# Two interleaved recurrent-memory transformer layers: full V passes for blocks 0, 1 and 14, spread weights copied from partition 64, and a new order of tasks

## The chip, the cores and the metric

The kernel runs on one NeuronCore of a Trainium2 chip. The metric is the device time of one execution in microseconds. The kernel before took 1785.24 us as the median of three runs (1784.02 to 1785.46). Engines are named as in the profile: PE is TensorE (PEld its weight loads), DVE VectorE, ACT ScalarE, POOL GpSimd, SP SyncE. SP and POOL mostly issue DMAs here.

## The reference

The input is one sequence of 2048 tokens of width 512, and the same layer is applied twice, with the same weights. A layer adds a recurrent-memory attention to its input, and then a gated feed-forward network (FFN). In the attention the sequence is cut into 64 segments of 32 tokens; 8 memory rows go ahead of each segment, and the attention's output for these rows is the memory of the next segment, so segments must follow one another.

```python
mem = mem0                                        # 8 x 512
for s in range(64):
    h = concat([mem, x[:, 32*s:32*s+32]], axis=1) # 40 rows, x after layernorm
    q, k, v = h @ Wq, h @ Wk, h @ Wv              # 32 heads of 128
    p = softmax(where(mask, q @ k.T * scale, -1e9))
    o = (p @ v) @ Wo
    mem = o[:, :8]; outs.append(o[:, 8:])
# one layer, applied twice:
x = x + attention(layernorm(x))
h = layernorm(x)
x = x + (sigmoid(h @ w_gate) * (h @ w_up)) @ w_down   # 512 -> 1792 -> 512
```

All inputs are bfloat16.

## The kernel before

**Steps.** Both layers run at once, the second six segments behind the first (`LAG` = 6), so that 70 steps do the whole work. In 58 of them both layers are present and every matmul of the step has 80 columns (40 rows of each layer); the 6 first and 6 last steps have one layer and 40 columns. A step (`emit_step`) goes through 32 heads in groups of six: Q and K (L890), their copy out of PSUM to `qku` (ACT), scores (L904), the mask added (DVE, L918), maximum, subtraction, exponential (ACT, L928), sum, reciprocal and product to `pb` (DVE, L923 to L935), a transpose on PE (L947), a spread of the transposed probabilities into `ptsb`, probabilities times V (PV, L973), a copy to `otsb` (ACT), and Wo (L991). At the end of the step DVE writes the new memory rows into the next step's `hT`, and ACT writes the segment's output to `oxT`.

**The spread.** A transposed pair of heads (u, 16 + u) lies in PSUM with the one head's keys at partitions 0 to 39 and the other's at 64 to 103. `ptsb` has for each pair two stretches of columns: stretch 0 is used with partitions 0 to 39, stretch 1 with partitions 64 to 103, and the rest of each is zero, so that one matmul takes both heads' keys at once. Stretch 0 is a plain copy of partitions 0 to 39. Stretch 1 is written on partitions 0 to 103, each multiplied by a scalar of its partition, `lower`, that is 0 below partition 64 and 1 from there on: on ACT an activation with a scale (L1222), on DVE a product (L1224). In a plain copy the lines are L1230 (ACT) and L1232 (DVE).

**V.** V of the memory rows and of the 8 last or first rows of a segment is computed inside the steps, as strips: 32 columns of `hT`, four matmuls side by side on PE (`strips`, L815). V of the other 24 rows of a segment doesn't depend on the memory and is computed ahead, for a block of 4 segments, written to DRAM (`scr`) and read back by the steps into `vsb`. A `v_pass` (L693) multiplies a tile of 128 columns by all of Wv in 32 matmuls of 512 columns; a block has only 96 such columns, so columns of other blocks fill up the rest. `v_half` (L730) does the same with 64 columns, two matmuls side by side; `v_strip` does it with 32 columns. Before the first steps `v_group` makes V of blocks 2, 14, 3, 4, 5, 7 and then 8, 10, 11, 13 of layer 0; what blocks 0 and 1 still need is made in between by one strip and one half (`trace`, L1150). In layer 1, a block's V is made when its FFN of layer 0 is done: `v_pass` with fillings from layer 0, but a half for block 14 and a strip for block 15. In the start the results are staged in nine buffers of the FFN's weight rings (`wd`, `wg`, `wu`: `bootp`), from which SP and POOL write them to DRAM (L1226).

**FFN.** When a block's four segments are done, `ffn` transposes `oxT` (L1061), adds the input, normalizes (`layernorm_T`, L642: statistics L649, transposes L662), and does gate and up (L1093), tanh (L1098), product (L1100) and down (L1117). Its weights are streamed from DRAM for each block by POOL (L1085, L1086, L1111).

**What sets the order.** `Kern` doesn't issue instructions but tasks, with an engine or a choice of ACT or DVE, a duration, and what they read and write. `Planner` plays them through with fixed costs and gives each engine the ready task of highest rank. The ranks are written out: a compressed list, `SEQUENCE` (L53 to L152), holds the rank of every task, and the lines that read it are

```python
for k, (q,) in enumerate(struct.iter_unpack("<H", code)):
    T[left.pop(q)].tail = -float(k)
```

So which of ACT and DVE does a copy, and in what order all engines work, comes from `SEQUENCE` and the planner's costs. PE tasks that the planner sees starting late get filler matmuls on the tile `hot` in front of them (`warm`, L416; issued at L1216); the first ones are at the start of the kernel. A semaphore wait stands only where data or a buffer demands it.

Of the kernel before, what the change touches and what calls it, by code (L numbers as in the profile page):

```python
# [53 lines left out]
;Aht@pIrb8fB#p5?Q#$k*OKvZZTq^c3OM%bV44b=*R*ZTyW=(F)eXpo=!dnjd%&eFWe?4v9B9J-6{(d-LCut;#!E)o@XKL;|1Yh}DX~>av(XnTcNY5yDmuUNDYpk)1hbP~Icf*@B%SY3<$N!PMdC+w  # L54
TzC*H?wh$B-*Ih~y~Z^1eU45ybkQ1*)!rl+2M7#!1kA=M>_00gM+A4yerPR?|M?Mj6^>>JOVW=CEf+cd3@>&Nfi0vId6NWR);FU?#N7i-E<e}?kQ5;smk7+$yR>6M$&vA+ka>GT!8=_b4-#fP#)eF7
^yFAVNqaBx;!Z*DxPH}w4u4hwLD|Xk-(55Lk^B_BDfkRj%d!v=C<*w7SG;+fg+&T)>)vE^_U=fY&kC>YwKQIya^N!=lH>FlpJ`Jr&lF|=A)fY+g;i{E@r#X;(VDk3V2MMXacuh+Y1k_asM6Wlyelal
#hat)UmCRL92k7baU(yGZ`~C!81W~7P5Erk>AYc<Vay?}YFcMj2ofpnp$(sP&YA3~nf~n+b1fFy?|Zym`QSa144a*IfxPvGj&Q1ek!IqLN$jiF41N6_7PG1D?N__fhI#wYegIrLSdO>RI&L#ADzYcB
9Qqa8r^xHgLyr2s6(Q^~qr%E_$NJ+TpJ_bc{R>AcDm>XZ4K<5#ddGdVwMU;&cRuZ|Sp~k`OZ$e|X_~sQ@384vzE1LEOy7FI`;?xf^#@MMQ)L6bC_!Zn4S4CHx9Vjn^H}pFj3R+|IJ2mzre;noNVd$S
`{%;vED%u54cw3M^F8VWNicF9{B~XUq?7A1595()pJ)9U7U(TRXvIYfie-lrSI2C)aZ1BBh3$_bQ;!I-B=8ScYh1ck&O!bB=K^(6{|r6Qx~A%7Guq$r@Iax)(DGfYMGmfWTtN`TiNx0^a_h-)zaQ;Y
Bg~_fxFI1YgW5VrkU}+v(OG0q+i!<|tAlPcRfvDusTf+wG<zAh-6L;+Y1?sI#2|g1{X&hwViH*}otG=?Uzck!7(XzcfK!b2s0y$`SNOr$pn;5(vR*N@6t6GIu9c&BiE<wNN?P(QqaXRd3M2ScK!LD`  # L60
7NE8fpYJ@UG|VxPeYSAG0la_&djDUlCG|bBoZOzAT#$(zHi(qOLpXAuXb5%<ke>jX1k1`o2(mU?ngq;3!G;hMQLm2&9MTEUYd^USvXFM#vQ$cKmjg>LrQvGCuN0;hmD;jcN{gk}oA#{rr~t7er6x;>
4TAPsm6b5FLH-g|Nf9h4giYb{D&c`|4)4`L+JTg9TM;~}=IotkUY(*Y!dPX~EqzNqLnvA&8*(y?XY|Ec+`KUE@_SSE)gkFi<&UF6JtvvpbP{*<I0G^z6$#&pA}^v95^Q4FK#<`jp&L`QSey9`{hytp
ep4|DPRnnzJfR5<$bbinu=f`jwczBNxe3uhZ<*z*5#J~4a?5s>6axJof)V}FxLuSWLQ`X$p%|GAo3ni>PtV+JzEAC$o%TiCe#d7B$K5bY%WL%|Y?`a4x@DA(YsP8dw{qC8hys!6@G=TJ3;?U)VFlx0
p<M<>KJllT(z)CRu8?`e3^R_R7%q?S32qi7rh98c7=(LFh!0=aD^hH1fNfXqg+Sja7$z4P_WGLKlHYlxk!E{x!eD5T8C@MZ?8P+s8nOs}&1S4ol`b-NnC>Xi=go6~%Yjg-4mHO!zq-ODIoX(~$HahI
@>xN0b)~I`DIDj5VKMa;CZ!v*mkbmOJ)#~W9x(W_v;<nswK`+PTq}ipg*!qKSltnE+$xw7Xt>R@wAQgZ(cg;enc1@7fR_`9(15bKuOa8wjwP|W7E?oWno808^?XT*fvZ96JauH_vO6Tmg0YAX{%<GP
x&vaN_I%f%_>nw(eGPl2kX+vA>jgyX^`O19337j8ctxfD{|+Geiw9%@3fRrZv?20mB-ZcAf?E$T01iSEPFlGkD*OepKVV{in{2e29t=mMTqiEZTBE&ID`7X6Mk+WhT~yUj_1`*B0!BsL3UYqo?S%Vq
U~wE&tp6ZiVbg<Vu#-btWwj?J)D@CYb1QP&m*#PL94pnFvBWYRVkl3T5;SG{PpgL>Y&7Ql1a;Xg%4O>TI04XhhFijc@Xaj9&%wm+O^!e2Is7ho@U?|Mv)s#Z>S-JQQ#^hP6vJ~o=FQdi%0==QiO4>}
e22-8{8_Hk?+)?_0!^US$Hin*eL}LmU1~LxfMwEBA4T-2y4BQI`Q`64rb)aYczym_%e@Wk1AuUFK%C=ysBJZCRbO!Y(YYGT<zd6Mwt&h>Ca^n2NDBRxQWx&kPPPClqibM>xRMi&j62;fUA|z^Rcv5p
F-MNEhkhZ`GG5|d;IIVWX3i~0UVC9j1JR_k)g}?mU=2&5>*Rm+{_7pfxv?)^BxJ;D;a}CKd+}lN*i{g!Cy29Nm6fs_s@A?29$S^C=sV2}7Gf8_q&p!Q-YYz<B<R6Q_L7&#1<{@t2|<x!)7#Viogyj%
#-k9m4_)fkps3Y)zWP9b))iXN6jc_5mj%JnzCGR%<`NT61>o}26adbxHKRWL;eGC_dPO$_0O%g3i&ylcjeO4Kp62wN^0l#G6AFX@sZ^p&lw_s>8|c<!RV%n$fDjRZ^Xo3)dI6V@-wLB+#PD@hFC|K{  # L70
hmxDVz+rV(-EotTD{>}bC$E+{l9$s&EXe`8-@_@{(5~Q9mF~S=mCXo-n@iGREv|B+hO}uaWNVIcBn--!6`yjXIwzk;tw$!|KNqC$<@Mh~wq+c2tXd(#Sr5!A-C=djQjW|zR>pY8ZsJpuHW?k&Vb2JQ
uK|mZtO+LXNgAg_(QsnAn`7TMhXkU87ogepo>y~+Q6YK~1|}aZxCTk*_)GF*LQIhh36&7b>}*Sf3aF_c%*8+#IpW86KlVU=PpvHDgCV0ph`o{zROB--HMhg)Z{yqq7Md>tmspIb4I7+>36}snbBa~p
2aq{FMm-sS@IOYq2mBa3IjrPDLfH_wb!L?PC1T|kd4ugY$iW8dl9Wn@+q#mR|8AO(pY8)gqHT0JZH)K^N=vOt<7^u-*$(l~x1U$PlUtaJALTr+N%)sKo=X09?|my^)5C^3SE4k&!$P)9kk;k6_2g=+
Xo<ZissDeGX{x7oi<<eTlp~=irUE^K35dz<U*p)9mm+d=#S6VL#4*xk?AUu>i@32H9Xk7!kk_K%&o5%^Sg@sug$7E7OfE13qWWUI<gX~Ww=Ovk<b`gMnA(LF)GbK-eGV(1eZq-0q2A1%j71R50jC+4
(YzP{LgPu!joT@AK^rRGm+vVYvgOLUd8rkU;M*n6fXUc#<4{U(<*Jw%^s|AolsW{O5e?q{R_5NdEk8h+662I+)Aqfs4y9uUn};G(N@<LuFs|^cT2FPBk6;o7V$@9XgP@*E$knBwHr>Rl>{fn#3`Kt?
yh8LxMxizaxtE9ijw|3QBSBOL8_*nr`Ija$bn=z6WE8x*$~+<;`&N15!cf9T9fLAG-W%WU!ZwOoz+`YmAGo$BFvfAhCU$wVm+!7~hqUD?_Qj=5pJZxrj>B%sT+T>^Mpe?7D7;6#U{20sx38&r-oZv<
@f;0J3*rnK+>gY7iHrU98Tc!cU$yG52J(53IMpe}CyZMp-M}xnkjatQP^<S=pQKx;v4)WilNu5`<Za2;cEYv!A-^%SNfLQcZHw<TrO#PTqr1ut(uD2lWlxw84HtnVFYJyK21!>3Pf#x4_<auBIOT|n
+@;+PE;I~5c;iLu7VSwLd!<@@giENcHgyQSL;-J2%c`n1>tw)5Bs}veFA<rH!^3m=l`VY}Nszs5V--R@?57p?P(+>mj+CH3TAIxks-M;?YeONKMhQ_kw+?5>kTJHu|7yVyF>aFUs;2k$08rksLjZ&}
Rec5D4v+VLqz!LXr1aXx264-a^;D{bA9Zt}4bb>Bb_oPv)r^`d2*V&n2Ps(kqh|OKVk6^jP`eI67p;O+<c~o`+;F|9sQaL-_ZCgX_3J6psL~YuH;xzf`)FU$t#f-U$eq7GKrs6{7FHkpW}34-RKFM*
9&x(UP}Ft7D%r_qN6h*20^EO0T}Wm?E1yp5ENr4Ju^T6EzeEMp)Bxm$T|rJ-CxTow#WGfD?k-in)T%Z8GRC)%u=eaRl_Ei`LMbFvL;YDLA~vt~$m$JHk6jxGBe&YFI+>Nh?*OuRiCPnCt@Nm2(HxK7  # L80
#&3kRM`t_Q;5~4|e>TMT4t<3*yUdt-xWMmna~NN*hW^#KJ3(n?D%%4`{Q+jJuR0q4-_lBy1j+FBqmip{O6sP`{bVE4hNzX|>QS_7B!LY(zVBx%^%(gHKijzO7Ss7Y(G2Y2VQ+E`6%mA5j&X?^I+)=|
P<db;>vgq@xzey}P_~g3{N0R$zl8UO=BM~MHCS_OrtXQ46onh0Y#OYaL!ZE2hoY+*G}tq}KBV|{#L!ZpbzLAaT=ge(F?IDIVMCq|mJBTHQ7CK5JO9=<=;)u%Yj;dLVc$R@gieZ`3AQh;6$rQ@iQZ@=
V>RB0haCzv329qrPHxI7KHybS8kD}@tey_pdZ+S3^+1!Zd_u(#@Bwc51(75!RI^zH@e*z62rR(bpoRk@rSm4S)S>3R3(Wmz*PCj{K$|na6?y2wU-w!(O%p6C9;oB8ZWV&<g-`Z^=HY<$y{^Z}jzCH3
UV$HD&VAwr6NtQ=vm`Xi+b-%FeG1g-5T&0ujXOTbNIQ{--zb|ZXytJtlj%7Tc{m1gKrfa#1X|V|As@F`7PH^zsG86&KLMk?>yZwc_JoAGr4WCLyeG~q5GD-oSX}2SSUvbPtzotDQV0E)5@I+Lha>C&
DS}ZGSn^mAJ`rlJm$5wePawoBajMO_l>j@?a2^U6_XSpq6S=J&H%kq4yvh*XzCIoZEU5NZczw6pMsmG}ABT=!bK@{MoQf~)lh)A0R22|G2BZt657mYk*_Tox-<g_09hV%;nL)YWonN|3AoDDx&1bL#
na*q83IB<G*_XVk%zy^teDZs~klOgm%HrUN2`M2h$pxj`RxaLf?mzW9jL{u4b|2D$NCMsLEnv^EJh#UKVL&G@cccOKTX~vm=xXk>U(k{q><I@&qD4ep%cxk8wmbLK%on{EPuT3?KiL3BsfB_s1}bzk
4k|w0K9P#^uUS|!0xaU$hu;r;-r3W&(`9`69^o6k9MDHHCCOPN>8OGEB7kEu=OXx}z3lSM@#1-PR{12eGz$@r>xDR@OeAgi{t+wvo>a0$WAP0PR9xFiZje_>iXPbTL!I&>UXu+LdY@e1wZR>E17rZB
_+1n?x+n@BHD(xyH5M3>DojQSVA(+cjxuKoi`As`(3r341mYa=<Gnp#T0tV^_cl4vhHpPKWj~AM*68j?JL({AjU)?K8UBd2%9vf(4s6E?TZ5#2(31QOu_voI?SmO95M~gstN^S&ygMVMa+7$!j~~*w
>n0u^sTKie_itwQlu@d`$Zj>onhtI!b0vvzI)BHLoRI$U?9LZM)w3v7pp8=Wpl7T(#6V4<Yi}9FIZDO+1savChV`Bwh!a{l%y(g|5;5s7w^124BDWWQHs3LPqOE<c0yvy1C^1zPbcI>H>xn!)3D3@R
0ejF8VuC8mkDGEa&ISH)g{aX_*WmOWBZF4(w=N*V^Q|3g%A^g5GeDl>1C_i%H2H#=*lDDJa2^QLXVdUf&jgBJXyA@u?p3@x%H%c$e0#Fu<fvQcuJ;TBqCnx9iYc^$QG7^^dbn&AkGoUyANwJZSqPhK  # L90
Ac>4^b;;ty(xTHUj2Jk&pY&#O3PT@VMEmFVd&dixCF6K<_$liKg3Cj*V%4jhO3@Wv#1C|H^oLjrm!TiSpn57#u77vrsh{=&Bkb^MTE8UmD`d-2n0-lFoX^MDTotFvOL_g{o`^VVLKK*p6%^F6_vHwy
L%E;$n_9PyS)iahe;p1n{}jFulI{!Q1ducj@Bbp282b;W9E58@b2ydomxZm{=_sh)pl*hMxqO1J>PY^+m4UKxeO8+f+8jLgrYvd@;1y27j3(5TF_=J=u{nd(<XyYI*}vjdwexVPNW<`~(nxQV`Q3bm
?-oKCugIcU$CVRPsibT<&C{`K8rw`m={?5dMI#P67pVd5XXX!^kt#O7jdXHtpC<=aQ_M-IF1c$;XZ^`K2CoLbmqR$Ivq{#PQJlH<ka(UMG@!Wy?g!OE;NF9YA=d6(hACy`S2&ca19}PpzuBXTH08Tu
@Lz?f1zQpJ>%+nhM7NU7yh@DH3;cUaFfmvXqEpg)AVAQFNWD5-cvZBj8C+?m#N=#2Gz`(7O!lBeMK#0m|1R1c7XDoN+Wi~qW$PQ}4iTimXzlVCmsLkEz@waJu_xEIADt!`c|AG5*imf6#OId*7Omc%
qaSm5>$72OwOoYELPh^-&@7Cs=@8jZsTMRf!amf|sTUxf>V*{4CGsTvibsUK&XTPA+hHsZ3PI1D<FlDN+@A@t933*jJ1!OX*s2Pp$90mq4+}v0yg#t*hCdVr+krL5Y2j14j40Fk8#jZ7N*okytgprx
RoHXPQ>sp|qSDHq>3xvdg;+6VhrdRa&E_m8?%9AM0TPy1JQMu{){ovpB9COdT^_c<EN`3f$n$c_`mRbTrd}lj^xn?M>P}XdptxnwQf0TIqV&^G9k3bqu^`cP>6-h=l3S1LvjFU*kOXblPG4e&Z--0E
+KhA|kTn<6k|h`R`SZ$l@Oss%2G~13Q-M0VSk1Z`OA9`BGJ=fH_Oc3Xv<Fj}eMi@iZ>m!MW2RF5Y@NbA;&M@_i@z@lO}~Tk2qmy$XZgEXy*xS3zgC_1$wK@jWjKs|ETZb2|0cV;KeBM8Uew32FhHk<
g2?JK%8cPAmwQ$OY6r?+a;<v(-M7Hlwh@ahq}H<85-$X?@JSbXE2?g5?(sr-a(*h{<wT>lJ=Q#V6#SmiIfE3+i=WW-Uc3Bi+M*W2C~08AQAXzaep+y0(7sVh)!;#B2t36^j}s4`QIIT`gP<(b<y}U;
# [361 lines left out]
class Kern:  # L460
# [91 lines left out]
    def setup_consts(self):  # L552
# [10 lines left out]
        nc.vector.memset(self.hot[:], 0.0)  # L563
        nc.vector.memset(self.negh[:], -0.5)
        nc.vector.memset(self.lower, 1.0)
        nc.vector.memset(self.lower[0:64], 0.0)

    def clear(self):

# [726 lines left out]
```

## Time and profile before

| what | value |
|---|---|
| median of three runs | 1785.24 us |
| the profiled execution's own time | 1784.02 us |
| its span | 1782.3 us |
| granted PE clock, mean | 0.999 |
| PE busy | 1754.4 us, 98% |
| ACT busy | 1166.1 us, 65% |
| DVE busy | 1142.3 us, 64% |
| POOL busy | 575.4 us, 32% |
| DMA share 0 to 14, 14 to 58, 80 to 130 us | 0.87, 1.02, 0.38 |
| DMA share 130 to 1655 us | 0.51 |

How to read it: an instruction group is given as line, engine, operation, output and input tile, sizes, and how often; then its busy time in us and the mean of one in ns; then the idle time of its engine in front of it and what ended that idle time. Matmuls are pipelined, so the mean of one (198 ns for 80 columns) isn't what it takes of PE's time; the distance from one start to the next is. The chain is the work that ended last, followed back through what released each step. The DMA share is the mean busy share of 16 DMA engines. Of V matmuls, the trace holds records of 388 with `xvl` and 211 with `xvf` of 448 and 224 that are issued: some matmul records are missing.

### The profile page before, as it was taken

What the parts mean: (1) busy time and instruction counts of PE and PEld (TensorE: products, weight loads), DVE (VectorE), ACT (ScalarE), POOL (GpSimd) and SP (SyncE); (2) the same over time, 40 slices, a digit from 0 to 9 for tenths busy, and PEclk for the clock granted to TensorE, in tenths of its full rate; (3) what the DMA queues carried; (4) which work ended last, traced back from release to release, by engine and by line L of the source; (5) the groups of instructions that cost most, each with busy time, mean ns of one, the idle gap of its engine ahead of it and who ended that gap; (6) DMA issues with size and microseconds to landing.
All of it is one profiled execution on the core that took longest, in us unless ns stands there. A gap on an engine that the chain in (4) does not pass through costs nothing.

```text
span 1782.3 us, 91985 instructions
## 1 busy us (share of the span) xinstructions
PE 1754.4 (98%) x39870; PEld 1518.0 (85%) x40077; DVE 1142.3 (64%) x3944; ACT 1166.1 (65%) x2960; POOL 575.4 (32%) x827
## 2 busy tenths in 40 slices
PE   9999999999999999999999999999999999999998
PEld 4588888988898898889898898988888888989886
DVE  4376666776677567756666676657656765666665
ACT  5676756666666667666666666666666666667564
POOL 4314031413233242323324231333324232333332
PEclk9999999999999999999999999999999999999999
DMA  9825254635555464445546453555555354554543
GB/s 322 278 80 154 70 153 121 185 107 156 156 161 152 133 176 127 140 144 165 159 128 199 135 155 105 162 160 166 157 147 172 109 146 140 158 156 145 158 144 94
DMA packets 138599, 270.66 MB, mean 152 GB/s; under 512 B 32954, under 2 KB 71746, under 8 KB 138194
## 3 DMA queue, kind: packets, MB, share of 16 engines
q0 software_dynamic: 56624, 181.91, 34.2%
q1 hardware_dynamic: 81570, 82.86, 16.3%
q8 instruction: 314, 5.14, 1.2%
q14 instruction: 91, 0.75, 0.1%
HBM read 220.41 MB, written 25.69 MB: 138 GB/s over the span
## 4 chain that ended last, share of the span: by engine, by line
PE 91%; DVE 5%; ACT 1%; issue 1%; DMA 1%; SPq 0%; POOL 0%; ACTq 0%; DVEq 0%; POOLq 0%
PE bank L890 32%; PE bank L991 16%; PE bank L1093 10%; PE bank L693 8%; PE bank L815 7%; PE bank L973 4%; PE bank L904 4%; PE bank L1117 4%; PE bank L947 2%; DVE st L918 1%; PE bank L1216 1%; PE bank L662 1%; DVE small L930 1%; DVE small L923 1%; DVE st L925 1%
## 5 line engine op out<-in xcount | busy, mean ns | idle before, releaser
L890 PE MATMUL bank<-hT,wq_sb 128*128 128x80 bf16 (+1 forms) x8960 | 621.8, 198 | 0.6
L890 PE MATMUL bank<-hT,wk_sb 128*128 128x80 bf16 (+1 forms) x8960 | 621.6, 198 | 0.6 <-issue 0.6
L1230 ACT CAST qku<-bank 128x480 bf16<-128x480 f32 (+3 forms) x770 | 388.5, 513 | 219.3 <-PE bank L890 137.9
L890 PEld LDWEIGHTS <-wq_sb 128*128 128x128 bf16 x8960 | 454.4, 99 | 34.0 <-issue 23.1
L890 PEld LDWEIGHTS <-wk_sb 128*128 128x128 bf16 x8960 | 450.8, 99 | 0.8 <-issue 0.7
L918 DVE TENSOR_TENSOR st<-bank,cst 40x240 f32<-40x240 f32 (+3 forms) x768 | 278.3, 368 | 186.0 <-PE bank L904 177.8
L991 PE MATMUL bank<-otsb,wo_sb 128*128 128x80 bf16 (+1 forms) x8960 | 363.6, 198 | 1.8 <-ACT otsb L1230 0.4
L991 PEld LDWEIGHTS <-wo_sb 128*128 128x128 bf16 x8960 | 336.9, 99 | 16.3 <-issue 2.0
L1230 ACT CAST otsb<-bank 128x480 bf16<-128x480 f32 (+3 forms) x420 | 199.8, 483 | 64.0 <-PE bank L973 51.0
L1086 POOL DMA_DIRECT2D wu<-in_B_w_up_dram x217 | 164.4, 758 | 239.1 <-PE bank L1093 96.2
L1085 POOL DMA_DIRECT2D wg<-in_B_w_gate_dram x217 | 164.4, 758 | 236.0 <-PE bank L1093 93.5
L1111 POOL DMA_DIRECT2D wd<-in_B_w_down_dram x217 | 154.2, 711 | 221.1 <-PE bank L904 90.4
L928 ACT ACTIVATE st<-st 80x240 f32<-80x240 f32 (+3 forms) x420 | 159.3, 381 | 37.2 <-DVE st L925 34.8
L652 POOL TENSOR_TENSOR small<-small,cst 128x1 f32<-128x1 f32 (+1 forms) x80 | 45.2, 567 | 427.6 <-DVE small L651 427.3
L1093 PE MATMUL bank<-xnT,wg 128*128 128x128 bf16 (+2 forms) x1784 | 171.6, 218 | 1.0
L1093 PE MATMUL bank<-xnT,wu 128*128 128x128 bf16 (+2 forms) x1784 | 171.0, 218 | 0.0
L930 DVE TENSOR_REDUCE small<-st 80x6 f32<-80x240 f32 (+3 forms) x420 | 150.9, 361 | 19.3 <-ACT st L928 16.7
L904 PE MATMUL bank<-qku 128*128 128x80 bf16 (+1 forms) x2240 | 159.9, 198 | 1.4 <-ACT st L928 0.2
L925 DVE TENSOR_TENSOR st<-st,small 80x240 f32<-80x240 f32 (+3 forms) x420 | 154.6, 369 | 3.1
L935 DVE TENSOR_TENSOR pb<-st,small 80x240 bf16<-80x240 f32 (+3 forms) x420 | 153.9, 369 | 4.0
L923 DVE TENSOR_REDUCE small<-st 80x6 f32<-80x240 f32 (+3 forms) x420 | 151.6, 362 | 4.1
L973 PE MATMUL bank<-ptsb,vsb 104*128 104x80 bf16 x2048 | 139.2, 199 | 1.7 <-ACT ptsb L1230 0.2
(103 smaller groups left out, 2344.6 us busy)
## 6 DMA issues: line engine op xcount, KB each, us to landing
wg<-in_B_w_gate_dram POOLq DMA_DIRECT2D x220, 256.0 KB, 4.3
wu<-in_B_w_up_dram POOLq DMA_DIRECT2D x220, 256.0 KB, 4.2
wd<-in_B_w_down_dram POOLq DMA_DIRECT2D x220, 256.0 KB, 4.3
vsb<-scr SPq DMA_DIRECT2D x460, 48.0 KB
vsb<-sst SPq DMA_DIRECT2D x464, 32.0 KB
scr<-vst SPq DMA_DIRECT2D x112, 96.0 KB
wv_sb<-in_A_Wv_dram SPq DMA_DIRECT2D x8, 512.0 KB
wq_sb<-in_A_Wq_dram SPq DMA_DIRECT2D x10, 384.0 KB
```

What stands on the lines that cost most here:

```text
L890: nc.tensor.matmul(o_ap, lhsT=W[:, c, h * P:(h + 1) * P], rhs=mv(c), start=(c == 0), stop=(c == DC - 1))
L904: nc.tensor.matmul(s_all(SB)[:, w0 + i, :], lhsT=fview(qku[:, i, 0, 0:1], [(1, P)]), rhs=qku[:, i, 1, 0:ncol], start=True, stop=True)
L918: pl.add("DVE", dve_ns(n, True), lambda gsz=gsz, hs=hs, st=st, SB=SB, pj_=pj_, npj_=npj_, mk=mk, idx=idx: nc.vector.tensor_tensor(out=st[p ...
L923: pl.add("DVE", dve_ns(n), lambda hs=hs, st=st, mx=mx: nc.vector.tensor_reduce(out=mx[pr, hs], in_=st[pr, hs], axis=AX.X, op=ALU.max), r=s ...
L925: pl.add("DVE", dve_ns(n), lambda gsz=gsz, hs=hs, st=st, mx=mx: nc.vector.tensor_tensor(out=st[pr, hs], in0=st[pr, hs], in1=mx[pr, hs].uns ...
L930: pl.add("DVE", dve_ns(n), lambda hs=hs, st=st, sm=sm: nc.vector.tensor_reduce(out=sm[pr, hs], in_=st[pr, hs], axis=AX.X, op=ALU.add), r=s ...
L973: nc.tensor.matmul(fview(OB[:, o:o + 1], [(ncol, 2), (1, L)]), lhsT=self.vsb[halves[u // 8]][0:64 + L, j, (u % 8) * P:(u % 8 + 1) * P], rh ...
L991: nc.tensor.matmul(WB[:, c * ncol:(c + 1) * ncol], lhsT=self.wo[:, h, c * P:(c + 1) * P], rhs=otsb[:, hl, 0:ncol], start=(h == 0 and c == ...
L1085: pl.add("POOL", 760, lambda wg=wg, fs=fs: nc.gpsimd.dma_start(out=wg[:], in_=self.wgv[:, :, fs]), r=[("wo", self.H - 1)], w=[gk] + bt, la ...
L1086: pl.add("POOL", 760, lambda wu=wu, fs=fs: nc.gpsimd.dma_start(out=wu[:], in_=self.wuv[:, :, fs]), r=[("wo", self.H - 1)], w=[uk] + bt, la ...
L1093: nc.tensor.matmul(gu[:, 2 * i + k, 0:n], lhsT=W[:, c, i * P:(i + 1) * P], rhs=xnT[:, c, rw], start=(c == 0), stop=(c == DC - 1))
L1230: nc.scalar.copy(out=dst, in_=src)
```

## The change

- `SEQUENCE` is replaced, so the order of the tasks on every engine is a new one. The planner's costs are the same in both files.
- The scaled write of stretch 1 of `ptsb` becomes a plain copy of partitions 64 to 103 only; `lower` goes. The lower partitions of that stretch stay zero from a write of zeros at the start of the kernel, which was there before.
- V of blocks 0 and 1 of layer 0 is made as a first `v_group`, with full passes, ahead of blocks 2 and 14; block 14 of layer 1 gets the full `v_pass` of the other blocks. `take_part`, `v_half` and `v_strip` go; the strip of block 15 stays and is written out in `ffn`.
- The memory's load and the layernorms of blocks 0 and 1 are made before the groups of V.
- Behind a piece of V weights three x blocks are loaded, not two. V weights come in eight pieces, two of them under way, in both kernels.
- The steps with one layer in which a step reads only 8 rows of V from DRAM and makes the others as strips (`thin`) are the first and last 4, not 6. So reads of 24 rows (`vsb` from `scr`) go from 460 to 476 and those of 8 rows from 48 to 32; strips' reads of one 64 KB form go from 48 to 32 and those of the 32 KB form from 464 to 480.
- Scalars of layernorms have three slots, not four.

In matmuls issued: V with 128 columns of `xvf` 224 to 256, of `xvl` 448 to 480; halves 64 to 0; strips of `xvl` 64 to 32; fillers from 103 records' worth to fewer (512 columns: 76 to 63 issued).

```diff
 SEQUENCE = r"""
...
@@ setup_tiles
-        small = c.tile([P, 60], F32, name="small")
-        self.lower = small[:, 58:59]
-        self.lns = [small[:, 10 * i:10 * i + 10] for i in range(4)]
+        small = c.tile([P, 48], F32, name="small")
+        self.lns = [small[:, 10 * i:10 * i + 10] for i in range(3)]
@@ load_weights
-            for b in xb[:2]:
+            for b in xb[:3]:
                 self.load_x(b, *self.boot_x[b])
-            xb = xb[2:]
+            xb = xb[3:]
@@ emit_step
                 def spread(i=i, nu=nu, ptsb=ptsb, PB=PB):
-                    r = slice(0, 64 * i + L)
+                    r = slice(64 * i, 64 * i + L)
                     pt = PB[r, 0:nu * LW // 2].bitcast(BF16).rearrange("p (u j q) -> p u j q", u=nu, j=2)
-                    dst = fview(ptsb[r, 0, i, 0:1], [(nj * LW, nu), (LW, nj), (1, L)])
-                    return (dst, pt[:, :, 0:nj, :]) + ((self.lower[r], "scaled") if i else ())
-
-                d = copy_ns(nu * nj * L, True)
-                d["ACT"] += 93.0 * i
-                pl.add(("ACT", "DVE"), d, spread, r=[PB], w=[("ptsb", pi, i)])
+                    return (fview(ptsb[r, 0, i, 0:1], [(nj * LW, nu), (LW, nj), (1, L)]), pt[:, :, 0:nj, :])
+
+                pl.add(("ACT", "DVE"), copy_ns(nu * nj * L, True), spread, r=[PB], w=[("ptsb", pi, i)])
@@ ffn
-                self.v_strip(lambda c: self.xvl[q][:, c, 0:32], [("xvl", q, 0)], 1, b, 2)
-                return
-            if b == self.NBLK - 2:
...
-                self.v_half(self.xvl[q], 0, [("xvl", q, 0), ("xvl", q, 1)], 1, b, 2, 0, 0)
+                sb = self.strips(lambda c: self.xvl[q][:, c, 0:32], [("xvl", q, 0)])
...
@@ trace
-        self.thin = (range(self.LAG), range(self.NSEG - self.LAG, self.NSEG))
+        self.thin = (range(BLK), range(self.NSEG - BLK, self.NSEG))
...
+        p0 = self.pre1(0)
+        p1 = self.pre1(1)
...
         self.load_x(2, *self.boot_x[2])
+        self.load_mem0()
         self.load_weights()
+        self.v_group([0, 1], {0: p0, 1: p1}, [[(0, 96, 0, 8)], [(0, 0, 0, 24)]])
         self.v_group([2, 14], {}, [[(0, 0, 0, 24)], [(0, 96, 0, 8)]])
         self.v_group([3, 4, 5, 7], {}, cuts)
-        self.load_mem0()
-        p0 = self.pre1(0)
-        p1 = self.pre1(1)
-        x0 = self.xvl[2]
-        self.take_v(*p0, 0, x0, [("xvl", 2, 0)], 0, 0, 8)
-        self.v_strip(lambda c: x0[:, c, 0:32], [("xvl", 2, 0)], 0, 0, 0)
-        self.take_v(*p1, 0, x0, [("xvl", 2, 1)], 64, 0, 8)
-        self.take_part(*p1, 0, x0, [("xvl", 2, 1)], 96, 8, 16, 2)
-        self.v_half(x0, 64, [("xvl", 2, 1)], 0, 1, 0, 8, 2, True)
         self.v_group([8, 10, 11, 13], {}, cuts)
```

## The prediction

> **What bounds the kernel now.** I read the page's busy shares and its chain first, then TensorE's timeline of the first 70 us, ScalarE's beside it, then the groups by line, and last VectorE's timeline from the middle of the run. The page:
>
> ```profile
> PE 1754.4 (98%) x39870; PEld 1518.0 (85%) x40077; DVE 1142.3 (64%) x3944; ACT 1166.1 (65%) x2960; POOL 575.4 (32%) x827
> ...
> PE 91%; DVE 5%; ACT 1%; issue 1%; DMA 1%; SPq 0%; POOL 0%; ACTq 0%; DVEq 0%; POOLq 0%
> ```
>
> TensorE is busy for 98% of the span and is 91% of the chain that ended last; the granted clock is full (0.999). So the sum is kept on TensorE: matmul time added or removed counts in full, and other engines count only where they make TensorE wait. Its timeline at the start (start us, duration us, then the instruction group; in brackets the idle time before it and what ended it):
>
> ```profile
> 13.46 1.90 PE L693 MATMUL bank<-wv_sb,xvf 128*128 128x512 bf16 x7
> ...
> 30.35 1.91 PE L815 MATMUL bank<-wv_sb,xvl 128*32 128x512 bf16 x32
> 32.20 1.90 PE L693 MATMUL bank<-wv_sb,xvf 128*128 128x512 bf16 x7
> 34.03 1.92 PE L730 MATMUL bank<-wv_sb,xvl 128*64 128x512 bf16 x16
> 35.88 7.94 PE L693 MATMUL bank<-wv_sb,xvf 128*128 128x512 bf16 x35
> 43.66 0.39 PE L662 MATMUL bank<-cst,xn 128*128 128x128 bf16 x4
> 43.88 4.48 PE L693 MATMUL bank<-wv_sb,xvf 128*128 128x512 bf16 x20
> 48.20 0.39 PE L662 MATMUL bank<-cst,xn 128*128 128x128 bf16 x4
> ...
> 52.01 6.22 PE L693 MATMUL bank<-wv_sb,xvf 128*128 128x512 bf16 x27
> 61.26 5.30 PE L693 MATMUL bank<-wv_sb,xvf 128*128 128x512 bf16 x16 [3.03 <-ACT wu L1230]
> ```
>
> Matmuls overlap, so a price is the distance from one group's start to the next's. A full V matmul: (48.20 - 43.88) / 20 = 0.216 us. A half one of 64 columns, two side by side: (35.88 - 34.03) / 16 = 0.116 us. A strip, four side by side: (32.20 - 30.35) / 32 = 0.058 us. The last line is the largest stall of the whole run: TensorE idles 3.03 us behind a copy on ScalarE, which itself had waited for a write of V to DRAM:
>
> ```profile
> 53.13 0.59 ACT L1230 CAST wd<-bank 128x512 bf16<-128x512 f32 x1 [0.30 <-DMA scr<-wg]
> 60.62 0.59 ACT L1230 CAST wu<-bank 128x512 bf16<-128x512 f32 x1 [6.91 <-DMA scr<-wu]
> ```
>
> In that stretch the DMA engines are saturated (from 14 to 58 us a share of 1.02 at 323 GB/s; from 80 us on 0.38). For the rest, from 130 to 1655 us TensorE is busy 1508.33 of 1525.00 us; counting by start-to-start distances against what the shapes stream in, its waits in the whole run come to some 50 us, nearly all of them under 0.7 us each.
>
> **The change, part by part.** The sum is made against the profiled execution: span 1782.3, its own time 1784.02, which is the lowest of three; the median, 1785.24, is 1.2 above it.
>
> *V of blocks 0, 1 and 14.* Full passes take the place of halves and strips. Counting both kernels' instructions: full V matmuls of the fillable kind go from 224 to 256 (blocks 0 and 1) and from 448 to 480 (block 14), halves from 64 to 0, strips on the xvl tile from 64 to 32. TensorE: + 64 x 0.216 = 13.8; - 64 x 0.116 = 7.4; - 32 x 0.058 = 1.9; together **+4.6 us**. At two and four side by side at no cost of switching, the removed ones would be 6.9 and 1.7 and the sum +5.2: that is the upper end. Copies out of PSUM change by a dozen on ACT and DVE (0.6 us each by the row above), which both engines have room for at 64 and 65%. The writes to DRAM on SP and POOL stay 64 at the start and grow by 0.26 MB, 0.8 us of saturated DMA at 323 GB/s.
>
> *Start.* The first V matmul, at 13.46, comes directly behind fillers. Before, it needs block 2, the first load; after, it needs blocks 0 and 1, and block 0 is the eighth load on SP, behind two pieces of V weights, a piece of Wq and four x blocks: 2.1 MB, 6.5 us at 323 GB/s. Before, the fifth load (1.5 MB) had its statistics start at 8.53. 0.6 MB more is 1.9 us: 10.4, and then the 4.9 us that the trace shows from statistics to first V matmul: 15.3. As its neighbours in the queue may land out of order, 13.5 is the other end. I take +1 (0 to +2). Three slots of layernorm scalars instead of four lie in the same chain and are inside this range; later, layernorms are some 15 us apart and the third slot is free again long before.
>
> *The stall at 58 us.* The staging buffer wu that ACT waits for is written again 3.5 us of TensorE work after its last use (and once 4.4 us, the 4.00 us wait of ACT at 42.44); every other slot has 9.3 or more. In the new order the shortest distance is 6.1 and the next 10.4. With a write under way for some 7 to 8 us behind saturated queues, 6.1 leaves 1 to 2 us of ACT waiting, most of it covered by banks in hand. I take **-2.5** (-3 to 0). If it goes, the DMA queues at a share of 1.02 are late next, with the extra 0.8 us; so no more than the 3.03 can be gained.
>
> *New order of tasks.* All small stalls are dealt anew. I counted in both instruction orders the TensorE work between the matmul that starts a chain on ACT and DVE and the matmul that waits for it, with chain lengths set so that the order of before gives its measured waits. Before to after: into the FFN's transposes (oxT, 24 waits with 11.1 us over TensorE and its loads) 8 to 10 of 33 blocks with nothing between, +1.1; into the transposes of the weights (pb) 5.2 to 8.3, +3.1; into scores, gate and up together +2.3; into Wo -1.0; into PV -0.4. Sum +5.1 at unchanged chain lengths; the count's own error is about 3. POOL's weight loads and SP's loads of V rows are reordered with the tasks; both queues have slack there (DMA share 0.51 from 130 to 1655), and the thin steps' changed strips and row loads add no more than 0.8 MB in 1700 us: nothing, unless a weight piece is issued late, when a stall like one of L1061's (0.5 to 0.7) follows.
>
> *The spread.* 420 instructions that write the second half of the probabilities lose their scaling and 64 of 104 partitions. The rows of both forms:
>
> ```profile
> L1222 ACT ACTIVATE ptsb<-bank,small 104x240 bf16<-104x240 bf16 (+3 forms) x266 | 112.8, 426 | 18.7 <-PE bank L947 16.6 <-DVE st L918 0.2
> ...
> L1230 ACT COPY ptsb<-bank 40x240 bf16<-40x240 bf16 (+3 forms) x269 | 83.7, 313 | 19.8 <-PE bank L947 16.9 <-DVE ptsb L1224 1.1 <-ACT th L1098 0.3
> ...
> L1224 DVE TENSOR_SCALAR ptsb<-bank,small 104x240 bf16<-104x240 bf16 (+3 forms) x154 | 47.1, 306 | 22.2 <-PE bank L947 18.4 <-ACT ptsb L1230 2.4
> ```
>
> ACT: 426 to 313, 0.113 us less on 275; DVE: 306 to 242 (the plain copy's row), 0.064 less on 145: 31 and 9 us less busy time. That is off TensorE's path but for the waits into PV, some 5 us in all; 0.1 shorter turns the -0.4 above into -2.9. The other end: all instructions of before on both engines start at partition 0 but for a handful, and the new spread starts at 64, which no row prices. What neighbours have today is an overlap:
>
> ```profile
> 700.83 0.39 DVE L930 TENSOR_REDUCE small<-st 80x6 f32<-80x240 f32 x1
> 701.14 0.40 DVE L925 TENSOR_TENSOR st<-st,small 80x240 f32<-80x240 f32 x1
> ```
>
> L925 starts 0.31 after L930, which takes 0.39: 0.08 of overlap, the median on DVE; on ACT it is 0.10. Were the overlap lost on both sides of every spread, DVE would pay 145 x 2 x 0.08 = 23 and ACT 275 x 2 x 0.10 = 55 us of time, in place of the 9 and 31 saved; both still fit beside TensorE, but pb and ptsb come 0.1 later in part of the groups: by the same count up to +4. Between -2.5 and +4 I take the stalls of both parts together as **+3** (-2 to +8).
>
> The page "VectorE: DVE Perf Modes" of the Trainium skill, section "Two Vector instructions with no wait between them", speaks against the change here: as I read it, an instruction that starts in another 32-partition group than the last one in that memory is held until every earlier Vector instruction has finished, and so is the next one that goes back. No row of before shows it. By it the DVE end above would be the true one (14 us net of DVE time more), and the sum would be about 1 us higher than without it; on ScalarE it says nothing.
>
> Sum: 1784.0 + 4.6 + 1 - 2.5 + 3 = 1790.1; with the 1.2 to the median, 1791.3. I say **1791**.
>
> **Rivals.**
>
> *Faster, by shorter spreads.* Place: the 420 groups' chain from the transposes to PV. The other terms come to +4.6 + 1 - 2.5 + 5.1 = +8.2; to end over 0.2% (3.6 us) below, 0.1 us must count in full in 118 groups of 420. At 140 groups: 1785.2 + 8.2 - 14 = 1779.4. For it: ACT and DVE wait 16.6 and 18.4 us for the transposes just ahead of the spreads, so the spread follows at once. Against it: waits into PV are only some 5 us today.
>
> *Within 0.2%: the start pays for the passes.* The stall goes wholly (-3), the first V matmul is not later (0), and the order is as good as before (-1): 1785.2 + 4.6 - 3 - 1 = 1785.8. For it: 1.8 of the added 4.6 lie in the DMA-bound start. Against it: block 14's part lies near 1600 us, where nothing hides it.
>
> *Much slower, by the start at partition 64.* Overlaps lost on both engines, +4 and a step of the recurrence late more often: 1791.3 + 5 = 1796 or more, up to 1800.
>
> *Start stall grows.* The added V writes make the boot writes late in more places, +3 instead of -2.5: about 1797.
>
> **How the numbers follow.** Forecast 0.53 (its own range 1787 to 1796), faster rival 0.12, within-0.2% rival 0.15, partition 64 0.13, start stall 0.07. A measurement of this kernel tells 0.2%, 3.6 us, from no change: faster is below 1781.7, slower above 1788.8. Of the forecast, 0.08 lies below 1788.8. Faster 0.12, same 0.23, slower 0.65. The range: low 1783, which leaves the faster rival out; high 1799, which takes in most of the two slow ones.
>
> **What would show it.** Right: L693 grows to 736 matmuls, L730 is gone; PE busy is about 5 us up; no gap over 1.5 us near 58; the spread on ACT falls to about 0.31 and on DVE to about 0.24 us. Wrong: a first V matmul after 16 us; a new gap of some us before 80; idle time in front of L973 or L947 up by more than 4 us; the instructions after a spread starting only at its end; or PE's idle from 130 to 1655 far from the 16.7 us of now.

## The result, and the profile after

The changed kernel takes 1805.62 us (median of four runs, 1805.13 to 1806.98), the kernel before 1785.35 beside it (four runs, the three above among them): a ratio of 1.0114, 95% interval 1.0097 to 1.0132. It is slower by 20 us, and 6.6 us above the top of the range. Later both ran again beside some of the experiments: 1808.08 to 1786.87, ratio 1.0117 (1.0102 to 1.0132).

Busy shares and chain, from the page of the kernel after:

```profile
span 1803.3 us, 91862 instructions
...
PE 1767.0 (98%) x39806; PEld 1523.7 (84%) x40031; DVE 1162.7 (64%) x3926; ACT 1185.7 (66%) x2980; POOL 573.6 (32%) x828
...
PE 86%; DVE 6%; ACT 4%; issue 2%; DMA 1%; SPq 1%; POOL 1%; POOLq 0%; ACTq 0%; DVEq 0%
```

The shares of busy time hardly move: TensorE 98%, VectorE 64%, ScalarE 66%. The chain tells more: TensorE 86% instead of 91%, and 4 points more for ACT and DVE together (10% instead of 6%).

The start went as worked out, as TensorE's timeline of the kernel after shows (start us, duration us, instruction group; in brackets the idle time before it):

```profile
14.72 0.87 PE L1158 MATMUL bank<-hot 128*128 128x512 bf16 x4
15.76 3.63 PE L690 MATMUL bank<-wv_sb,xvf 128*128 128x512 bf16 x15 [0.17 <-ACT xvf L1166]
...
55.34 1.03 PE L690 MATMUL bank<-wv_sb,xvf 128*128 128x512 bf16 x3
56.39 0.40 PE L659 MATMUL bank<-cst,xn 128*128 128x128 bf16 x4
56.62 5.56 PE L690 MATMUL bank<-wv_sb,xvf 128*128 128x512 bf16 x25
```

The first V matmul is at 15.76 instead of 13.46, and the stall of 3.03 us near 58 is gone; it stands in all six profiled runs of the old order, those of the experiments included, and in none of the eight of the new one. At the end of the first step the kernel is 2.5 us ahead of the one before.

Where the time goes is seen from the moments at which ACT writes a segment's output (128 such writes; difference to the kernel before, each from one profiled execution):

| write | before, us | after minus before, us |
|---|---|---|
| 1 | 86.1 | -2.5 |
| 13 | 279.2 | +0.3 |
| 49 | 736.0 | +6.3 |
| 97 | 1347.4 | +14.8 |
| 115 | 1576.7 | +17.8 |
| 119 (behind block 14's pass) | 1626.9 | +19.9 |
| 128 | 1765.9 | +21.0 |

Between 280 and 1577 us it loses 17.5 us at an even pace, about 1.3 us in every 100. No single event does that. TensorE's groups that wait for the spread and for what follows it, before:

```profile
L991 PE MATMUL bank<-otsb,wo_sb 128*128 128x80 bf16 (+1 forms) x8960 | 363.6, 198 | 1.8 <-ACT otsb L1230 0.4
...
L973 PE MATMUL bank<-ptsb,vsb 104*128 104x80 bf16 x2048 | 139.2, 199 | 1.7 <-ACT ptsb L1230 0.2
```

and after, with the spread's copies:

```profile
L940 PE MATMUL bank<-otsb,wo_sb 128*128 128x80 bf16 (+1 forms) x8960 | 364.5, 198 | 3.3 <-ACT otsb L1166 2.0
...
L1166 ACT COPY ptsb<-bank 40x240 bf16<-40x240 bf16 (+3 forms) x562 | 178.7, 320 | 39.5 <-PE bank L899 30.4 <-DVE ptsb L1168 1.0
...
L922 PE MATMUL bank<-ptsb,vsb 104*128 104x80 bf16 x2048 | 140.9, 199 | 6.7 <-DMA vsb<-sst 1.7 <-ACT ptsb L1166 1.4 <-DVE ptsb L1168 0.7
...
L1168 DVE COPY ptsb<-bank 40x240 bf16<-40x240 bf16 (+3 forms) x278 | 69.1, 249 | 46.5 <-PE bank L899 37.3 <-ACT ptsb L1166 4.7 <-PE bank L856 0.2
```

TensorE's idle time in front of PV grows from 1.7 to 6.7 us, in front of Wo from 1.8 to 3.3. Gaps shorter than the modelled ends of matmuls don't show in these columns. By the distance of starts against what the shapes stream in, between 130 and 1655 us, waits into PV go from 6.0 to 15.5 us, into Wo from 5.2 to 9.2 and into the transposes (pb) from 5.8 to 7.1; over all instructions they go from 69.5 to 90.0, which holds the records that are missing in both traces. Yet the instructions of the spread became shorter, as forecast: 320 ns on ACT (321 for the second stretch alone) in place of 426 for the scaled one, 249 on DVE (256) in place of 306.

### The profile page after: what moved, and what is told of

It is laid out like the page before. It is cut to its first block, busy times and chain, and to the rows that moved or that the text cites. A ratio compares the mean times of both kernels' runs of the same rounds, so it can differ in the third digit from the quotient of the medians.

```text
span 1803.3 us, 91862 instructions
## 1 busy us (share of the span) xinstructions
PE 1767.0 (98%) x39806; PEld 1523.7 (84%) x40031; DVE 1162.7 (64%) x3926; ACT 1185.7 (66%) x2980; POOL 573.6 (32%) x828
## 4 chain that ended last, share of the span: by engine, by line
PE 86%; DVE 6%; ACT 4%; issue 2%; DMA 1%; SPq 1%; POOL 1%; POOLq 0%; ACTq 0%; DVEq 0%
PE bank L842 30%; PE bank L940 15%; PE bank L1042 10%; PE bank L690 8%; PE bank L767 7%; PE bank L922 4%; PE bank L856 4%; PE bank L1066 3%; PE bank L899 2%; ACT ptsb L1166 1%; DVE st L870 1%; DMA vsb<-sst 1%; PE bank L659 1%; DVE small L882 1%; DVE pb L887 1%
## 5 line engine op out<-in xcount | busy, mean ns | idle before, releaser
L870 DVE TENSOR_TENSOR st<-bank,cst 40x240 f32<-40x240 f32 (+3 forms) x768 | 279.2, 368 | 220.1 <-PE bank L856 206.8
L1166 ACT COPY ptsb<-bank 40x240 bf16<-40x240 bf16 (+3 forms) x562 | 178.7, 320 | 39.5 <-PE bank L899 30.4
L880 ACT ACTIVATE st<-st 80x240 f32<-80x240 f32 (+3 forms) x420 | 159.4, 381 | 47.6 <-DVE st L877 43.8
```

Of the source, the lines that this page charges most:

```text
L870: pl.add("DVE", dve_ns(n, True), lambda gsz=gsz, hs=hs, st=st, SB=SB, pj_=pj_, npj_=npj_, mk=mk, idx=idx: nc.vector.tensor_tensor(out=st[p ...
L880: pl.add("ACT", act_ns(n), lambda hs=hs, st=st: nc.scalar.activation(out=st[pr, hs], in_=st[pr, hs], func=ACTF.Exp, scale=self.scale), r=s ...
L1166: nc.scalar.copy(out=dst, in_=src)
```

## The experiments

Theory A: the start at partition 64 costs time around the spread. Theory B: the new order of tasks and the added passes do. All ratios are to the kernel before on the same chip; the runs were on several chips, on which the kernel before took 1785 to 1788 us.

### The spread and the order, crossed

The changed kernel with the old spread; the planner's costs stay, so the order of the instructions is that of the changed kernel:

```diff
-                    r = slice(64 * i, 64 * i + L)
+                    r = slice(0, 64 * i + L)
...
-                    return (fview(ptsb[r, 0, i, 0:1], [(nj * LW, nu), (LW, nj), (1, L)]), pt[:, :, 0:nj, :])
+                    dst = fview(ptsb[r, 0, i, 0:1], [(nj * LW, nu), (LW, nj), (1, L)])
+                    return (dst, pt[:, :, 0:nj, :]) + ((self.lower[r], "scaled") if i else ())
...
```

> The changed kernel, its order of instructions as it is, with the second stretch of the spread written as before: partitions 0 to 103, scaled. Theory A (the start at partition 64 makes its neighbours wait): 1789 to 1794 us, that is 12 to 16 of the 20 us back; waits into PV fall from 15.5 to about 6 us between 130 and 1655. Theory B (the new order of tasks is worse, and the added passes): 1802 to 1807, the spread's form matters by no more than 3.

The kernel before with the new spread, in its own order:

```diff
-                    r = slice(0, 64 * i + L)
+                    r = slice(64 * i, 64 * i + L)
...
-                    return (dst, pt[:, :, 0:nj, :]) + ((self.lower[r], "scaled") if i else ())
+                    return (dst, pt[:, :, 0:nj, :])
```

> The kernel before, its order of instructions as it is, with the second stretch as a plain copy of partitions 64 to 103. Theory A: 1797 to 1802, the same 12 to 16 us lost without any new order. Theory B: 1783 to 1787, a shorter spread can only help an order that was good.

Both orders with a plain copy from partition 0, of 104 partitions (the edit of the changed kernel; in the kernel before, only the scaling is left out):

```diff
-                    r = slice(64 * i, 64 * i + L)
+                    r = slice(0, 64 * i + L)
```

> The changed kernel with the second stretch as a plain copy of partitions 0 to 103: the scaling is left out, so that the first head's probabilities stand in the second stretch too and the output is another. It has the start at partition 0 without the scaling's longer instruction. Theory A: as with the scaling or up to 3 us less, 1787 to 1794. Theory B: 1802 to 1806.

> The kernel before with the same plain copy of partitions 0 to 103 (scaling left out, the output is another). It prices what the shorter instruction alone is worth, 0.113 us of ACT and 0.064 of DVE, without any start at 64. Prediction's count: 2.5 us less, 1783; if the spread is off the path, 1785.

| second stretch of the spread | order and passes of before | order and passes of after |
|---|---|---|
| plain, from partition 0 | 0.9982 (0.9972 to 0.9992), 1785.58 us | 0.9989 (0.9979 to 0.9999), 1786.13 us |
| scaled, from partition 0 | 1 | 1.0018 (1.0009 to 1.0028), 1791.20 us |
| plain, from partition 64 | 1.0061 (1.0046 to 1.0076), 1799.58 us | 1.0114, 1.0117 |

Theory A holds, in both orders: the start at 64 costs 14 us against the plain copy from 0 in the old order (0.0079 of 1787) and 22 to 23 in the new one; against the scaled one 11 and 17. With the plain copy from 0 the two orders, passes included, are equal to what this can tell (0.0007). The scaling costs more than the expected 3 us in the new order, 5 where the old order pays 3, though that difference lies inside the intervals. So the order alone isn't bad; it takes the start at 64 worse, by some 8 us more than the old order, which is clear of them. One expectation of the old spread in the new order failed: waits into PV fell to 10.6 us, not to about 6.

### What the start at 64 does

In the changed kernel ScalarE's timeline shows a spread's two halves (x2), an exponential (L880) and a tanh (L1047):

```profile
705.77 0.40 ACT L880 ACTIVATE st<-st 80x240 f32<-80x240 f32 x1
706.22 0.72 ACT L1166 COPY ptsb<-bank 40x240 bf16<-40x240 bf16 x2
706.97 0.40 ACT L880 ACTIVATE st<-st 80x240 f32<-80x240 f32 x1
707.39 0.38 ACT L1047 ACTIVATE th<-bank 128x256 f32<-128x256 f32 x1
```

The same instructions in the changed kernel with the scaled spread (here the exponential is L883, the tanh L1051):

```profile
702.86 0.40 ACT L883 ACTIVATE st<-st 80x240 f32<-80x240 f32 x1
703.31 0.35 ACT L1176 COPY ptsb<-bank 40x240 bf16<-40x240 bf16 x1
703.57 0.45 ACT L1168 ACTIVATE ptsb<-bank,small 104x240 bf16<-104x240 bf16 x1
703.92 0.39 ACT L883 ACTIVATE st<-st 80x240 f32<-80x240 f32 x1
704.21 0.37 ACT L1051 ACTIVATE th<-bank 128x256 f32<-128x256 f32 x1
```

With the scaled spread every instruction from the second half of the spread on starts 0.1 before the last one's end: spread to exponential 0.61 us, to tanh 0.90. With the start at 64 the two copies of 0.35 follow one another without overlap (0.72 for both), the exponential starts 0.03 after them, and the tanh 0.02 after the exponential: 0.75 and 1.17. The exponential reads and writes SBUF only and is held by its write; the tanh is the first to read PSUM from partition 0 again, and is held in its turn.

Call a start held when another start partition keeps it back until the instruction before it has ended. I sorted all neighbours that follow at once (next start less than 25 ns after the last end) by one question: does the instruction read PSUM, or write, from another start partition than the last one that did so on its engine? Medians of the next start minus the last end, changed kernel:

| engine | same starts | another start | how many of the latter |
|---|---|---|---|
| ACT | -95 to -103 ns | +12 to +24 ns | 363 |
| DVE | -60 to -78 ns | +13 to +14 ns | 107 |

No group of neighbours breaks this, the pairs of two spreads at 64 included (7 on ACT, not held, -95 ns). The limit of 25 ns is narrow: another 122 neighbours with another start on ACT follow 25 or 26 ns after the last end and another 150 on DVE 30 to 33 ns after, most of them instructions that wait for a semaphore too. Up to 35 ns there are 485 on ACT and 257 on DVE, and none of these starts before the last end. So one held start costs 0.11 to 0.13 us on ScalarE and 0.09 to 0.11 on VectorE. This is the rule of the Trainium skill's page "VectorE: DVE Perf Modes", section "Two Vector instructions with no wait between them", and it agrees on VectorE; ScalarE, of which that section says nothing, behaves in the same way here.

Which engine's holds matter, by leaving the start at 64 to one of them:

```diff
...
+                    if tk.on != "ACT":   # the other kernel: "DVE"
+                        (nc.scalar.copy if tk.on == "ACT" else nc.vector.tensor_copy)(out=dst[64:64 + L], in_=src[64:64 + L])
...
```

> The changed kernel and its order; ScalarE writes the second stretch scaled from partition 0 (275 times), VectorE copies from partition 64 (145 times). If only VectorE holds instructions (all that the cited page states), the loss stays with it: 1803 to 1807 with the kernel before at 1787. If ScalarE holds too, most of the loss goes, as ScalarE does two thirds of the spreads: 1793 to 1797.

> The reverse: VectorE scaled from partition 0, ScalarE from partition 64. If only VectorE holds: 1789 to 1792. If ScalarE holds too, in proportion to the number of spreads: 1799 to 1803. The two losses of this run and of the one with VectorE alone should add up to the 17 us between the changed kernel and the one with the old spread.

At 64 on VectorE alone 1797.72 us, 1.0055 (1.0040 to 1.0070); on ScalarE alone 1801.83 us, 1.0083 (1.0068 to 1.0098). Against 1.0018 that is 6.6 and 11.6 us, together 18.2, as much as both at once (17). The first is just above its expected 1793 to 1797. Both engines hold; per spread it is 46 and 42 ns of kernel time.

Whether the read or the write does it, with the old order (the two kernels differ in the first added line):

```diff
-                    r = slice(0, 64 * i + L)
+                    r, rd = slice(64 * i, 64 * i + L), slice(0, L)    # read at 0, write at 64
+                    r, rd = slice(0, L), slice(64 * i, 64 * i + L)    # read at 64, write at 0
-                    pt = PB[r, 0:nu * LW // 2].bitcast(BF16).rearrange("p (u j q) -> p u j q", u=nu, j=2)
+                    pt = PB[rd, 0:nu * LW // 2].bitcast(BF16).rearrange("p (u j q) -> p u j q", u=nu, j=2)
...
-                    return (dst, pt[:, :, 0:nj, :]) + ((self.lower[r], "scaled") if i else ())
+                    return (dst, pt[:, :, 0:nj, :])
```

> The kernel before and its order; the second stretch is a plain copy that reads PSUM partitions 0 to 39 and writes SBUF partitions 64 to 103 (the second head gets the first head's probabilities, so the output is another). Only the write changes its start. If either side's change holds an instruction: as with both at 64, 1.0061 of before (1796 to 1800 with the kernel before at 1788), gaps of +12 to +24 ns around it. If only the read counts: 0.998 of before, as the plain copy from 0.

> The reverse: it reads PSUM partitions 64 to 103 and writes SBUF partitions 0 to 39 of the second stretch (the second head's keys are left out of PV, so the output is another). If either side's change holds: 1.0061 of before again. If only the write counts: 0.998.

1794.99 us, 1.0046 (1.0031 to 1.0061), and 1795.57 us, 1.0049 (1.0034 to 1.0064): either side is enough. Both stay a little below 1.0061, within its interval (1.0046 at its edge), and the traces show somewhat fewer held neighbours: up to 35 ns 423 and 416 on ACT against 456 with both sides at 64, 239 and 226 on DVE against 268. Where only the read is at 64, an instruction behind the spread that doesn't read PSUM isn't held (-96 ns on ACT, -78 on DVE); where only the write is, it is (+24 on ACT).

### Is it the hold, or simply engine time?

The held starts are worth at most 485 x 0.12 + 107 x 0.09 + 150 x 0.11, some 84 us, on engines that are busy two thirds of the time; what the engines lose by them in fact is in the table below, 67. A kernel without any start at 64, but with both stretches scaled, loses about as much time in longer instructions (the edit is that of the changed kernel with the old spread, but for this line and a column of ones):

```diff
-                    return (dst, pt[:, :, 0:nj, :]) + ((self.lower[r], "scaled") if i else ())
+                    return (dst, pt[:, :, 0:nj, :]) + ((self.lower if i else self.ones)[r], "scaled")
```

> The changed kernel and its order with no start at 64 anywhere, but both stretches scaled (the first by ones): longer instructions in place of held ones. Engine time over the plain copy from 0: ScalarE +21 for the second stretch and about +21 for the first, VectorE +9 and +8, together some 59 us; the changed kernel has 68 (44 and 24). If engine time is what costs, however it is lost: 59/68 of the 22 us between the two, +19, so 1.009 to 1.010 of before. If a held start costs beyond its time: as the scaling costs now (5 us for 30), +10, so 1.004 to 1.005 of before.

> The changed kernel as it is, on the same chip as the runs beside it, to have its distance to the kernel before there: 1.0114 as measured first (1805 to 1809 with the kernel before at 1785 to 1788).

It takes 1803.67 us, 1.0097 (1.0080 to 1.0114): engine time is what costs. The spread's groups of the plain copy from 0, and of this kernel:

```profile
L1166 ACT COPY ptsb<-bank 104x240 bf16<-104x240 bf16 (+7 forms) x562 | 155.0, 321 | 38.0 <-PE bank L899 34.2 <-DVE ptsb L1168 0.7
...
L1168 DVE COPY ptsb<-bank 104x240 bf16<-104x240 bf16 (+7 forms) x278 | 58.5, 240 | 51.6 <-PE bank L899 44.1 <-ACT ptsb L1166 5.3 <-ACT st L880 0.3
```

```profile
L1170 ACT ACTIVATE ptsb<-bank,small 104x240 bf16<-104x240 bf16 (+7 forms) x562 | 210.2, 421 | 33.1 <-PE bank L904 29.1 <-DVE ptsb L1172 1.0 <-ACT otsb L1178 0.2
...
L1172 DVE TENSOR_SCALAR ptsb<-bank,small 104x240 bf16<-104x240 bf16 (+7 forms) x278 | 75.1, 300 | 48.3 <-PE bank L904 40.8 <-ACT ptsb L1170 5.6 <-PE bank L861 0.3
```

0.1 us more on each of 562 spreads on ACT and 0.06 on 278 on DVE. Set beside the time in which ACT and DVE run or hold (their busy time, with pauses of up to 25 ns counted in):

| kernel, order of after | ACT, us | DVE, us | both over the first | ratio | us over the first | share |
|---|---|---|---|---|---|---|
| plain from 0 | 1150.8 | 1140.6 | 0 | 0.9989 | 0 | |
| second stretch scaled | 1171.9 | 1149.7 | 30 | 1.0018 | 5.2 | 0.17 |
| both scaled | 1193.6 | 1158.0 | 60 | 1.0097 | 19.3 | 0.32 |
| plain from 64 (second run) | 1194.0 | 1164.7 | 67 | 1.0117 | 22.9 | 0.34 |

In the old order the same reckoning gives 28 us for the scaling and 3.2 lost (0.11), and 64 us for the start at 64 and 14 lost (0.22). With pauses of up to 35 ns counted in, the start at 64 comes to 73 us in the new order and 68 in the old one (shares 0.31 and 0.21), and the other rows stay. So of every us that the two engines lose, however they lose it, TensorE's path pays a tenth to a third, more where more is lost (0.17 against 0.32), and for the start at 64 more in the new order. Waits into PV between 130 and 1655 us follow suit in that order, but for the last: 7.8, 10.6, 17.1 and 16.2 us down the table.

### The added passes

The changed kernel with the old spread, and half of the matmuls of the two new passes left out:

```diff
...
-                for c in range(DC):
-                    nc.tensor.matmul(B[:, :], lhsT=tile[:, c, :], rhs=self.wv[:, c, cs], start=(c == 0), stop=(c == DC - 1))
+                few = DC // 2 if any((j, b) in ((1, 14), (0, 0), (0, 1)) for _, j, b, _, _ in pieces) else DC
+                for c in range(few):
+                    nc.tensor.matmul(B[:, :], lhsT=tile[:, c, :], rhs=self.wv[:, c, cs], start=(c == 0), stop=(c == few - 1))
...
```

> The changed kernel with the old spread, and in the first pass of blocks 0 and 1 and in the pass of block 14 only 16 of the 32 matmuls (the second half of the contraction is left out, so these blocks' V is another). 32 matmuls less of 0.216 us. If added matmul time counts in full: 6.9 us less than with all (3.5 at the start, 3.5 near 1600 us). If the start hides the first pass: 3.5 us less, all of it near 1600 us.

1785.77 us, 0.9994 (0.9985 to 1.0004): 4.3 us less by the ratios, whose intervals leave some 2 us to either side, so between the 6.9 and the 3.5 of the two cases, and the ratios alone don't tell which. The two traces place it: 4.3 us less at the first write of a segment's output, 2.5 more between writes 115 and 119, where block 14's pass lies, 7.1 in the spans (the profiled run with all matmuls lies 1.8 above its median, the other at it). In both the first V matmul starts alike, at 16.77 and 16.83, and in the seven profiled runs of this order with all matmuls the first write lies between 82.9 and 85.6, against 81.25 here. By these traces the start does not hide its half.

### A faster version

The plain copy from 0 is worth 3.2 us, but mixes two heads. If the second stretch holds both, PV gives the sum of two heads' outputs there, and the sum is put right in Wo: o_u Wo_u + o_v Wo_v = o_u (Wo_u - Wo_v) + (o_u + o_v) Wo_v. The kernel before, with that difference made on VectorE behind the first step:

```diff
-                    return (dst, pt[:, :, 0:nj, :]) + ((self.lower[r], "scaled") if i else ())
+                    return (dst, pt[:, :, 0:nj, :]) + ((self.lower[r], "scaled") if i and t == 0 else ())
...
+                    if t == 0:
+                        for u in range(self.HH):
+                            nc.vector.tensor_tensor(out=self.wo[:, u, :], in0=self.wo[:, u, :], in1=self.wo[:, self.HH + u, :], op=ALU.subtract)
```

> A candidate for a faster kernel: the kernel before, in which from the second step on the second stretch is a plain copy of partitions 0 to 103, so that PV gives the sum of two heads there, and Wo of the first head has had Wo of the second subtracted from it by 16 VectorE instructions behind the first step. Same result as the reference's up to rounding. By the plain copy's run: 3 us less than before; the 16 instructions, 16 x 0.34 us at a time when VectorE has some 5 us free, may take 1 of it. 1784 to 1787 with the kernel before at 1788.

1786.04 us to 1787.64, 0.9989 (0.9979 to 0.9999). It beats the kernel before by 0.1%, barely clear of its interval, and the changed one by 1.2%. In its trace the second write of a segment's output comes 20.8 us after the first, in the other five profiled runs of this order 18.7 to 19.3: some 1.5 to 2 us that go with the 16 instructions and take back much of the gain.

## Why the prediction was wrong

The direction was right, the size was not: 1791 said, with 1799 as the top, and 1805.6 measured.

**The step that failed** is the last one of the spread's part: "both still fit beside TensorE, but pb and ptsb come 0.1 later in part of the groups: by the same count up to +4". What went ahead of it was sound. Two held starts for each spread, 290 on DVE and 550 on ACT, were 257 and 485 in the trace; the overlap lost was priced at 0.08 and 0.10 us and measured 0.09 to 0.11 and 0.12; the net loss of engine time against the scaled form, 14 us on DVE and 24 on ACT, measured 15 and 22 (from the two profiles, 1149.7 to 1164.7 and 1171.9 to 1194.0). But 17 us came through to the end for those 37, where +4 was the bound. And of its own bounds, -2.5 and +4, the sum took nearly the best: +3 for both parts beside +5.1 for the order leaves -2.1 for the spread. I took the busy shares of 64 and 65% for room. In each group the chain from scores to Wo passes ACT and DVE many times, on queues in order, and a held start delays everything queued behind it, not only pb and ptsb; my count moved two of the chain's links and left the others where they were. Waits into Wo, which I had going down by 1.0, went up by 4. Two of the signs of being wrong that the prediction names came: idle time in front of PV up by more than 4 us (1.7 to 6.7), and instructions behind a spread that start only at its end.

The rival "much slower, by the start at partition 64" was the case that came, at a price of +5 for what cost 17 to 22, and with a chance of 0.13. The cited rule was weighed at 1 us. On VectorE, of which it speaks, it was right, and the start at 64 on VectorE alone cost 6.6 us; on ScalarE, on which the prediction says that the page is silent, it cost 11.6.

**The rest of the sum** was too high, and that hid part of the miss: passes, start, stall and order came to +8.2, and with the scaled spread, where all of them are in and the start at 64 is not, they measured 3.2 (1.6 to 5.0). With 17 for the spread in its place the same sum would have given 1785.2 + 8.2 + 17 = 1810.4. That the range was left by only 6.6 us is luck in that part.

**Faster, by shorter spreads**: the shorter instruction alone is worth 3.2 us in the old order, near the 2.5 of the count, and 5.2 in the new one; both are far from the 12 that the rival needed.

**V of blocks 0, 1 and 14**, +4.6: 32 full matmuls left out, 6.9 us at the price used, gave 4.3 back, with some 2 us to either side. So added matmul time reached the end in large part, but that it counts in full isn't shown, and no run put the removed halves and strips back.

**Start**: first V matmul +2.3 us against +1 (0 to +2), with 15.3 worked out and 15.76 measured; the stall -3.0 against -2.5. Both together -0.7 against -1.5. The first V matmul varies, 13.4 to 14.6 us in the profiled runs of the old order and 15.1 to 16.8 in those of the new one. With the start's part of the added matmuls (32 x 0.216 - 32 x 0.116 - 32 x 0.058 = 1.3, not the 1.8 of the second rival) the measured two make +0.6 at the first write, where the kernel was 2.5 us ahead. A part of this the prediction left out: behind the stall the granted clock of the kernel before is 0.91 from 60 to 80 us, by estimate 20 x 0.09 = 1.8 us, and 1.00 in the kernel after. It is 0.91 there in four of the six profiled runs of the old order and 1.00 in all eight of the new one. The other 1.3 us are open.

**New order**, +5.1 at unchanged chain lengths: with the scaled spread the trace loses 5.1 us between writes 13 and 97 (+0.9 to +6.0 against the profile before). But the spans of these two executions differ by 8.7 us, where the ratio of medians says 3.2; with the plain copy, two executions on one chip differ by 2.0 between the same writes. Over the whole kernel order and passes together cost 3.2 us with the scaled spread and about 1.3 with the plain one. So 5.1 isn't shown and is more likely too high; what the term missed is that the new order pays more for the start at 64.

What stays open: which of the terms beside the spread's was too high, and why the share of engine time that reaches the end grows with the time lost and, for the start at 64, is larger in the new order. That it does is measured; that queues in order and tight distances make it so is argued.

## What to carry to other kernels

Room on an engine is, by these runs, not its idle share but the slack of the chain that passes through it: where TensorE follows ACT and DVE every fraction of a us, multiply the engine time that an edit adds by a measured share (0.1 to 0.35 here), not by nearly zero. An access pattern that alternates its start partition, on the read or on the write side, takes the overlap from two instructions at a time, now and then three, on ScalarE as on VectorE; a longer instruction that starts where the others start can be the cheaper one. And an order planned for one set of durations should be judged with those durations: crossing it with the instruction forms, four kernels, tells what either is worth.

## What the runs showed of the hardware

- ScalarE overlaps back-to-back instructions by 0.10 us and VectorE by 0.08; both lose it when the start partition of the PSUM read or of the write differs from the last one's (next start +12 to +26 ns after the last end instead of -103 on ACT; +13 to +14, or +30 to +33 with most of those that wait for a semaphore too, instead of -76 on DVE).
- The hold follows the memory, not the neighbour: an instruction that doesn't read PSUM passes unheld behind a read at 64 (-96 ns on ACT, -78 on DVE), and the next one that reads PSUM from 0 is held instead. Behind a write at 64 it is held (+24 ns on ACT).
- A copy of 104 partitions takes as long as one of 40 (medians in the changed kernel with the plain copy from 0: 355 against 352 ns on ACT for 240 elements, 269 against 266 on DVE); the scaling on top takes 0.10 us on ACT and 0.06 on DVE.
